# Five places instead of six for the weights of a layer change, and a V half that stays on the chip

## The chip, the cores and the metric

One core of a Trainium2 chip runs the kernel. The metric is the device time of one execution in microseconds (us), lower is better. Three runs of the kernel before gave 176.09, 176.46 and 176.43 us, a median of 176.43. One further execution was taken with the hardware profiler; it took 176.3 us, of which the instructions span 174.6 us. All times of single instructions come from that execution and are counted from the start of its span.

Five engines work side by side: TensorE (PE, matmuls; the profile shows its weight loads as PEld), VectorE (DVE), ScalarE (ACT), GpSimd (POOL) and SyncE (SP), which here only issues the transfers from the chip's main memory (HBM). The on-chip memories are SBUF, where loads land, and PSUM, eight banks that hold the results of matmuls.

## The reference

One token for each of 4 sequences goes through four layers: attention A, gated network B, then A and B again **with the same weights and the same cache**. Cut to what matters:

```python
def A(x):                               # x: 4 x 1 x 512
    q = (x @ wq)                        # 512 x 4096: 32 heads of 128
    k, v = last 2048 keys of each of 8 kv heads (4 query heads share one)
    p = softmax(q k^T / sqrt(128))
    return (p v) @ wo                   # 4096 x 512
def B(x):
    return (sigmoid(x @ w_gate) * (x @ w_up)) @ w_down   # 512 x 1792, 1792 x 512

x = x + A(layernorm(x)); x = x + B(layernorm(x))
x = x + A(layernorm(x)); x = x + B(layernorm(x))
```

K and V are 16 MB each (bf16), wq and wo 4 MB each, the three B matrices 1.75 MB each.

## The kernel before, in words

**Memory.** SBUF is cut into 50 half tiles of 512 KB (128 partitions x 2048 bf16). All of K, 32 half tiles, stays from the first attention to the second, so K is read once. The other 18 half tiles are a pool of nine whole tiles for V, wq, wo and the B weights. A tile of V holds one kv head for two of the four sequences: it is named by the head and by the pair, (head, 0) or (head, 1). The 2048 keys of a sequence lie 32 on each of 64 partitions; so each half of a V tile has 16 key blocks, 128 elements wide, on every partition.

**The two attentions.** The first (`attn_first`) takes the heads 0 to 7, the second (`attn_second`) 7 to 0, so that the last tiles of V can serve both. (7, 0) and (7, 1) do; (6, 1) waits in four PSUM banks meanwhile (`stash`, line 580, and `load_stash`, line 595, both transposes on DVE). The rest of V is loaded again.

**The layer change.** Between the two attentions lie the first B and the projection of q. Their weights are 18 loads of 256 to 512 KB: four quarters each of w_gate and w_up (448 KB), four parts of w_down (384 to 512 KB), and six of the eight 512 KB parts of wq, written (quarter of the rows, half of the columns); two parts of wq stay from the first attention. The pool has no free tile then, since wo's four tiles and V are held. So these loads go into **places**, half tiles that the first attention has just left:

- WQ and WR: the tiles that held the first two row quarters of wq. Their second halves keep the wq parts that stay. The first halves, (WQ, 0) and (WR, 0), then hold the two halves of the V tile (6, 0).
- Y: the tile of (6, 1), empty after the stash: (Y, 0) and (Y, 1).
- Z: the tile of (7, 0); its first half waits in PSUM in the meantime (`stash_half`, line 602) and so (Z, 0) is empty.
- SP: half a tile's worth of small buffers (`side`), not needed in between.

A load is named with its place by `load_half` (line 505 to 516). `load_wq`, `load_glu` and `load_v` list the loads in order. All transfers are issued on SP, in exactly that order (line 400): a load waits there until the last reader of its place is done, and those behind it wait too. The order of instructions on the other engines is made by a planner (`_schedule`) from estimated durations; behind the second norm, TensorE's order is fixed as written.

**V tile (6, 0).** In the first attention its half 0 is in (WQ, 0), half 1 in (WR, 0). Of half 0, 11 of the 16 key blocks are put aside: 7 in a PSUM bank as f32 pairs (`save_part`, a DVE transpose, line 639), 4 in the buffer of a constant, `permo` (`save_rest`, an ACT copy, line 644). For the second attention, `restore_part` brings them into (WR, 1) by an ACT copy and a DVE transpose (lines 650 and 652), and GpSimd builds the constant anew (line 658). The other 5 blocks of half 0 (160 KB, the load named `PART`) and the whole half 1 (512 KB) are loaded again.

**Fillers.** `keep_op` and `add_zeros` (lines 783 ff.) issue matmuls that add nothing to what is read later. They stand where TensorE would wait.

**The end.** In the last B (`glu` with `last=True`), two w_gate tiles and two w_up tiles are multiplied (line 1484), DVE transposes the result (1496), ACT and DVE form the gate, and w_down is multiplied in three pieces (line 1533). `x_rows` puts x into the same PSUM bank ahead of that (line 1468).

Of the kernel before, what the change touches and what calls it, by code (L numbers as in the profile page):

```python
# [6 lines left out]
F32 = mybir.dt.float32  # L7
BF16 = mybir.dt.bfloat16
ACTF = mybir.ActivationFunctionType
ALU = mybir.AluOpType  # L10
# [268 lines left out]
def build(nc, A_x, A_k, A_v, A_wq, A_wo, B_wg, B_wu, B_wd, out, cfg=None):  # L279
# [14 lines left out]
    REP = HQ // HKV  # L294
# [30 lines left out]
    with es:  # L325
# [99 lines left out]
        WR = ("wq", 1, 0)  # L425
        RET = ("ret",)
        PART = ("Vh", 0, HKV - 2, 0, 1)
        SP = ("side",)
        base = {SP: SIDE}

# [95 lines left out]
        def load_wq(k):  # L526
            if k == 0:
                for c in range(NC):
                    load(("wq", c, k), 2, "bw_8k", (2 * SLOT, wq_d[:, c, :], False))
            else:  # L530
                for c, i, place in ((2, 1, (WR, 0)), (3, 1, (Y, 0)), (0, 0, (SP, 0)), (1, 0, (Y, 1)), (2, 0, (WQ, 0)), (3, 0, (Z, 0))):
                    load_half(("wq", c, k, i), wq_d[:, c, i * SLOT:(i + 1) * SLOT], "bw_4k", SLOT, place)

        def wq_part(k, c, i):
# [21 lines left out]
        def load_glu(k):  # L556
            for nm, src, two in (("wg", wg_d, wg_p), ("wu", wu_d, wu_p)):
                if k == 0:
                    for c in range(NC):
                        load_half((nm, c, k), src[:, c, :], "bw_3k", F,  # L560
                                  (((WR, 0), (Y, 0), (SP, 0), (Y, 1)), ((WQ, 0), (Z, 0), (WR, 0), (Y, 0)))[nm == "wu"][c])
                    continue
                for cc in range(NC // 2):
                    load((nm, cc, k), 2, "bw_8k", (2 * F, two[:, cc, :], False))
            for n, (a, b) in enumerate(bounds_of(k)):
                if k == 0:
                    load_half(("wd", a, k), wd_d[:, a:b, :].rearrange("p k n -> p (k n)"), "bw_4k", (b - a) * D,
                              ((SP, 0), (Y, 1), (WQ, 0), (Z, 0))[n])
# [44 lines left out]

        def load_v(h, bp, k, n_use):
            name = ("V", h, bp, k)
            tiles = ({(HKV - 2, 0): ((WR, 1), (WR, 0)), (HKV - 3, 1): ((Y, 0), (Y, 1))} if k
                     else {(HKV - 2, 0): ((WQ, 0), (WR, 0))}).get((h, bp))
            if tiles is not None:
                halves[h, bp] = []
                for n, tile in enumerate(tiles):  # L620
                    half = ("Vh", n, h, bp, k)
                    load_half(half, pair_d(A_v, h, bp)[:, :, n * SLOT:(n + 1) * SLOT], "bw_4k", SLOT, tile, SAVED if half == PART else 0)
# [12 lines left out]
        def saved_f(s):  # L635
            return slot_ap(s)[:, SAVED_S:SAVED].bitcast(F32)

        def save_part(s):
            P.op("vector", "sv1", c_dve(SAVED_P), lambda v: v.transpose(saved_p, saved_f(s)),
                 r=[("slot", s)], w=[("sv", 1)], banks=(CB,))  # L640

        def save_rest(after):
            s = base[WQ]
            P.op("scalar", "sv0", c_act(SAVED_S), lambda a: a.copy(permo[:, :], slot_ap(s)[:, 0:SAVED_S]),
                 r=[("slot", s)], w=[("permo",)], after=after)
            give(s)

        def restore_part():
# [3 lines left out]
            b = P.op("vector", "rv1", c_dve(SAVED_P), lambda v: v.transpose(saved_f(s), saved_p),  # L652
                     r=[("sv", 1)], w=[("rv", 1)], banks=(CB,), after=tuple(fresh))
            for o in (a, b):
                o.deps.update(saved["deps"])
            for m in range(REP):
                P.op("gpsimd", "permo2%d" % m, 300.0,
                     lambda g, m=m: g.affine_select(permo[:, m * 128:(m + 1) * 128].rearrange("p (r v) -> p r v", r=REP),
                                                    one[:, 0:1].broadcast_to([128, 128]).rearrange("p (r v) -> p r v", r=REP),
                                                    [[0, REP], [-4, 32]], ALU.is_equal, 0.0, base=-m, channel_multiplier=1),  # L660
                     r=[("one",)], w=[("permo",)])

        on_free[Y] = lambda s: hfree.update((s, s + 1))

# [139 lines left out]
        def layer_norm(tag, b0, b1, for_q, add=None):  # L804
# [362 lines left out]
        def pv_wide(tag, h, k2, tiles):  # L1167
# [6 lines left out]
            def e_pv(pe):  # L1174
                last = None
                for n in range(4):
# [5 lines left out]
                                         src.rearrange("p (m t d) -> p t m d", t=2, d=128)[:, t], start=(n == 0), stop=(n == 3))  # L1182
                return last
            P.op("tensor", "PV" + tag, 16 * tm["pe_row"], e_pv,
                 r=[("slot", x) for x in ss.values()] + [("e", k2)] + [("rv", n) for n in range(2) if h == HKV - 2],
                 w=[("pso", k2, 0), ("pso", k2, 1)], banks=(ob,))
            for bp, _ in tiles:
                for name in sorted(set(x[0] for x in parts[bp]), key=str):
# [111 lines left out]
        def attn_first():  # L1300
            def front(h):
                k_transpose(h)
                softmax_unit("0.%d" % h, h)
                turn = lambda: turn_p(0, "0.%d" % h, h % 2, PBS[h % 2])
                return turn

            for h in range(2):
                front(h)()
            for h in range(HKV):
                tag = "0.%d" % h  # L1310
                turn = front(h + 2) if h + 2 < HKV else None
                if h == HKV - 1:
                    need(Z)
                    so0 = stash_half(0, named("oq0.%d" % (h - 1)))
                op = pv_unit(tag, h, h % 2, v_tiles[(0, h)])
                if h == HKV - 2:
                    oe, oq = named("oe" + tag), named("oq" + tag)
                    oe[0].deps.add(stash(stashed, (0, 1)))
                    oq[0].deps.add(stash(stashed, (2,), oe))
                    st = stash(stashed, (3,), oq)  # L1320
                if h == HKV - 1:
                    named("oe" + tag)[0].deps.update((st, so0))
                    for o in P.ops:
# [3 lines left out]
                    save_rest(tuple(named("pm" + tag)))  # L1327
# [117 lines left out]
        def glu(k, b0, b1, add=None, last=False):  # L1445
# [29 lines left out]
            for n, nm in enumerate(("wg", "wu")):  # L1475
                for c in range(NC):
# [3 lines left out]
                    def e_g(pe, c=c, s=s, n=n):  # L1480
                        last = None
                        src = slot_ap(s) if k == 0 else tile_ap(s)[:, c % 2 * F:(c % 2 + 1) * F]
                        for g in range(4):
                            last = pe.matmul(ps[32 * g:32 * g + NB, gub[n], 0:NF], xn[:, c * NB:(c + 1) * NB],  # L1484
                                             src[:, g * NF:(g + 1) * NF], start=(c == 0), stop=(c == NC - 1),
                                             skip_group_check=True)
# [210 lines left out]
```

## Time and profile before

| what | value |
|---|---|
| median of 3 runs | 176.43 us (176.09 to 176.46) |
| the profiled execution | 176.3 us |
| its span | 174.6 us |
| PE, DVE, ACT, POOL busy | 114.9, 105.9, 34.0, 23.1 us |
| bytes read from HBM | 69.37 MB |
| stretches of the span | first attention to about 105 us, layer change to about 122, second attention to about 162, last B to the end |

The page of the profile gives busy time by engine, the busy share in 40 slices of the span (one digit each, 9 is 90% or more; a slice is 4.4 us), the DMA queues, and groups of instructions by line. Further views used below: the chain of waits (the work that ended last, followed back; start, length, what), the timeline (start, length, engine, line, operation, output<-input, and in brackets the idle time before it and what ended that), the view by stretches (busy us and number of instructions by engine, granted TensorE clock, share of the DMA engines' time, GB/s), and the DMA view, which gives the time from a load's issue to its landing.

### The profile page before, as it was taken

How to read it: one execution, taken by the hardware profiler on the slowest of the kernel's cores; microseconds unless marked ns; L12 is line 12 of the kernel's file. 1: busy time of each engine (PE TensorE's matmuls, PEld its weight loads, DVE VectorE, ACT ScalarE, POOL GpSimd, SP SyncE). 2: the span in 40 equal slices, each digit the busy share in tenths (PEclk: the TensorE clock that was granted, in tenths of full speed). 3: DMA queues.
4: the chain of work that ended last, by engine and by line, in shares of the span. 5: the costliest groups of instructions: out<-in, count | busy, mean ns of one | idle time of the engine just before them, and what ended most of it. 6: DMA issues, size and time to landing. Idle time of an engine off the chain costs nothing.

```text
span 174.6 us, 3997 instructions
## 1 busy us (share of the span) xinstructions
PE 114.9 (66%) x1686; PEld 58.6 (34%) x1698; DVE 105.9 (61%) x262; ACT 34.0 (19%) x89; POOL 23.1 (13%) x92
## 2 busy tenths in 40 slices
PE   0536237167557092569788788767958999879853
PEld 0203012013434051243467552243323434446311
DVE  6407997994866938469323732316598999751531
ACT  2002022312212103011021010102233545430101
POOL 6100010101100101001010000002011543442000
PEclk9999999999999999999999999999999999999975
DMA  5999999999999999999999999999999999999970
GB/s 189 420 428 430 422 420 420 408 423 420 420 419 409 424 420 420 420 412 421 420 408 425 412 395 407 407 409 405 407 413 417 422 417 420 417 424 420 415 319 26
DMA packets 12370, 69.64 MB, mean 399 GB/s; under 512 B 1336, under 2 KB 1472, under 8 KB 6336
## 3 DMA queue, kind: packets, MB, share of 16 engines
q1 hardware_dynamic: 12344, 69.38, 97.0%
q8 instruction: 13, 0.21, 0.5%
q14 instruction: 5, 0.04, 0.1%
q10 hardware_dynamic: 8, 0.00, 0.0%
HBM read 69.37 MB, written 0.00 MB: 397 GB/s over the span
## 4 chain that ended last, share of the span: by engine, by line
DMA 71%; PE 11%; DVE 7%; SPq 6%; issue 1%; ACT 1%; POOL 0%; DVEq 0%
DMA arena<-in_A_v_cache_dram 49%; DMA arena<-in_B_w_down_dram 15%; SPq L400 6%; DMA side<-in_A_wq_dram 4%; DMA arena<-in_B_w_up_dram 4%; PE ps L783 2%; PE ps L1088 2%; DVE arena L595 1%; PE ps L986 1%; PE ps L1091 1%; PE ps L1181 1%; DVE small L1001 1%; ACT side L1016 1%; PE ps L1289 1%; DVE arena L1191 1%
## 5 line engine op out<-in xcount | busy, mean ns | idle before, releaser
L956 DVE STREAM_TRANSPOSE arena<-arena 128x1024 f32<-128x1024 f32 x32 | 37.0, 1205 | 0.1
L986 PE MATMUL ps<-arena,side 128*32 128x512 bf16 x256 | 23.3, 494 | 0.3
L1001 DVE TENSOR_REDUCE small<-ps 128x1 f32<-128x512 f32 x16 | 10.9, 679 | 15.8 <-PE ps L986 15.8
L783 PE MATMUL ps<-perm 128*128 128x448 bf16 (+1 forms) x65 | 18.5, 397 | 1.0 <-DVE side L1496 0.8
L1016 ACT ACTIVATE side<-ps,small 128x512 bf16<-128x512 f32 x16 | 11.0, 687 | 35.7 <-PE ps L1115 18.5
L973 PE MATMUL ps<-small,perm 128*128 128x512 bf16 x16 | 7.7, 482 | 12.0 <-DVE arena L956 11.3
L1088 PE MATMUL ps<-side,arena 128*128 128x64 bf16 x320 | 11.3, 192 | 4.0 <-DMA arena<-in_A_v_cache_dram 4.0
L1091 PE MATMUL ps<-side,arena 128*128 128x8 bf16 x256 | 8.1, 168 | 8.8 <-DMA arena<-in_A_v_cache_dram 8.7
L949 ACT CAST side<-ps 128x256 bf16<-128x256 f32 x16 | 5.9, 371 | 33.6 <-PE ps L986 26.6
L1088 PEld LDWEIGHTS ps<-side,arena 128*128 128x128 bf16 x320 | 10.2, 97 | 6.3 <-DMA arena<-in_A_v_cache_dram 6.3
L1031 ACT CAST side<-ps 128x512 bf16<-128x512 f32 x16 | 9.4, 587 | 12.6 <-PE ps L1289 2.9
L1045 POOL CAST small<-small 128x1 bf16<-128x1 f32 x9 | 1.7, 188 | 76.0 <-ACT side L1016 76.0
L1091 PEld LDWEIGHTS ps<-side,arena 128*128 128x128 bf16 x256 | 7.4, 104 | 11.6 <-DMA arena<-in_A_v_cache_dram 9.0
L986 PEld LDWEIGHTS ps<-arena,side 128*32 128x32 bf16 x256 | 6.3, 108 | 11.7 <-issue 8.7
L897 PE MATMUL ps<-arena,xn 128*4 128x512 bf16 x60 | 6.5, 498 | 4.2 <-DMA arena<-in_A_wq_dram 4.2
L1105 DVE TENSOR_TENSOR onb<-ps,rinv 128x16 bf16<-128x16 f32 x9 | 1.7, 185 | 11.4 <-PE ps L1088 10.8
L944 PE MATMUL ps<-side,eyew 32*128 32x64 bf16 x64 | 5.4, 212 | 4.3 <-ACT side L949 2.4
L1036 DVE STREAM_TRANSPOSE side<-side 128x256 f32<-128x256 f32 x16 | 6.9, 433 | 2.0 <-ACT side L1031 1.8
L1181 PE MATMUL ps<-arena,side 128*32 128x512 bf16 x112 | 7.3, 380 | 0.8 <-ACT side L1016 0.4
L783 PEld LDWEIGHTS ps<-perm 128*128 128x128 bf16 x65 | 5.9, 110 | 5.3 <-issue 2.9
L1496 DVE STREAM_TRANSPOSE side<-ps 128x448 f32<-128x448 f32 x4 | 2.6, 651 | 7.9 <-PE ps L1484 7.9
L1484 PE MATMUL ps<-arena,xn 128*4 128x448 bf16 x60 | 4.7, 360 | 3.1 <-DMA arena<-in_B_w_up_dram 2.7
(138 smaller groups left out, 151.1 us busy)
## 6 DMA issues: line engine op xcount, KB each, us to landing
arena<-in_A_v_cache_dram SPq DMA_DIRECT2D x26, 1024.0 KB, 16.6
arena<-in_A_k_cache_dram SPq DMA_DIRECT2D x16, 1024.0 KB, 24.9
arena<-in_A_wq_dram SPq DMA_DIRECT2D x4, 1024.0 KB, 7.8
arena<-in_A_wo_dram SPq DMA_DIRECT2D x3, 1024.0 KB, 26.6
arena<-in_A_v_cache_dram SPq DMA_DIRECT2D x5, 512.0 KB, 8.6
arena<-in_A_wq_dram SPq DMA_DIRECT2D x5, 512.0 KB, 6.7
arena<-in_B_w_up_dram SPq DMA_DIRECT2D x4, 448.0 KB, 6.1
arena<-in_B_w_gate_dram SPq DMA_DIRECT2D x2, 896.0 KB, 20.7
```

What stands on the lines that cost most here:

```text
L400: o = P.op("sync", name, 0.0, lambda e, dst=dst, src=src: e.dma_start(dst, src), r=r, w=w, dma_bytes=nbytes, dma_rate=tm[rate])
L783: last = pe.matmul(dst, weights, src, start=False, stop=False, skip_group_check=True)
L956: P.op("vector", "T%d_%d" % (h, t), c_dve(1024), lambda v, v32=v32: v.transpose(v32, v32), r=[("slot", 4 * h + t)], w=[("slot", 4 * h + t)])
L973: last = pe.matmul(ps[:, bank, :], perm[:, :], msk_m[:, :].unsqueeze(1).broadcast_to([128, 256, 2]), start=True, stop=False)
L986: last = pe.matmul(ps[32 * gi:32 * gi + 32, bank, :], qbd[:, q0:q0 + 32], kt[:, cp // 2, cp % 2, jh * NJ:(jh + 1) * NJ, :], start=False, s ...
L1001: lambda v: v.tensor_reduce(nmax[:, k2:k2 + 1], ps[:, bank, :], AXX, ALU.max),
L1016: lambda a: a.activation(prow[:, :].rearrange("p (m x t) -> p m x t", x=32, t=2), ps[:, bank, :].rearrange("p (m t x) -> p m x t", x=32, t ...
L1031: P.op("scalar", "pc" + tag, c_act(512), lambda a: a.copy(prow[:, :], ps[:, pb, :]), r=[("ppb", pb)], w=[("prow",)], banks=(pb,))
L1036: P.op("vector", "pt" + tag, c_dve(256), lambda v: v.transpose(et, prow[:, :].bitcast(F32)), r=[("prow",)], w=[("e", k2)])
L1088: last = pe.matmul(ps[:, ob, o:o + 64], v, ef[:, j % 2, at - at % 64:at - at % 64 + 64], start=(j == 0), stop=(j == 2 * NJ - 1), skip_grou ...
L1091: last = pe.matmul(ps[:, ob, bp * 8:bp * 8 + 8], v, ev[:, j % 2, j % 16 // 2, x0:x0 + 8], start=(j == 0), stop=(j == 2 * NJ - 1))
L1181: last = pe.matmul(ps[32 * g:32 * g + 32, ob, :], ew[:, g, mq, t], src.rearrange("p (m t d) -> p t m d", t=2, d=128)[:, t], start=(n == 0) ...
```

## The change

The places of the layer change are dealt anew, five instead of six: (WR, 0) is no longer among them. Half 1 of the V tile (6, 0) stays in it from the first attention to the second (`KEPT`) and isn't loaded again. Of half 0, only what goes into PSUM is put aside, 480 f32 columns instead of 448, which is 7.5 key blocks instead of 11; the copy into `permo` and back, and the rebuilding of `permo`, are gone. The `PART` load grows accordingly and is put into the list one place earlier, ahead of the last wq part. The halves of the V tile (5, 1) get other places. Some filler matmuls are added, dropped or moved.

```diff
         PART = ("Vh", 0, HKV - 2, 0, 1)
+        KEPT = ("Vh", 1, HKV - 2, 0, 0)
...
-                for c, i, place in ((2, 1, (WR, 0)), (3, 1, (Y, 0)), (0, 0, (SP, 0)), (1, 0, (Y, 1)), (2, 0, (WQ, 0)), (3, 0, (Z, 0))):
+                for c, i, place in ((2, 1, (Y, 1)), (3, 1, (SP, 0)), (0, 0, (Z, 0)), (1, 0, (WQ, 0)), (2, 0, (Y, 0)), (3, 0, (Y, 1))):
+                    if place == (Y, 1) and i == 0:
+                        load_half(PART, pair_d(A_v, HKV - 2, 0)[:, :, 0:SLOT], "bw_4k", SLOT, (WR, 1), SAVED)
                     load_half(("wq", c, k, i), wq_d[:, c, i * SLOT:(i + 1) * SLOT], "bw_4k", SLOT, place)
...
-                                  (((WR, 0), (Y, 0), (SP, 0), (Y, 1)), ((WQ, 0), (Z, 0), (WR, 0), (Y, 0)))[nm == "wu"][c])
+                                  (((WQ, 0), (Y, 0), (Y, 1), (SP, 0)), ((Z, 0), (WQ, 0), (Y, 0), (Y, 1)))[nm == "wu"][c])
...
-                              ((SP, 0), (Y, 1), (WQ, 0), (Z, 0))[n])
+                              ((SP, 0), (Z, 0), (WQ, 0), (Y, 0))[n])
...
+            if k and (h, bp) == (HKV - 2, 0):
+                halves[h, bp] = [(PART, 0), (KEPT, 0)]
+                return
-            tiles = ({(HKV - 2, 0): ((WR, 1), (WR, 0)), (HKV - 3, 1): ((Y, 0), (Y, 1))} if k
+            tiles = ({(HKV - 3, 1): ((Z, 0), (WQ, 0))} if k
...
-        SAVED_S, SAVED_P = REP * 128, 7 * 64
-        SAVED = SAVED_S + 2 * SAVED_P
+        SAVED_P = 480
+        SAVED = 2 * SAVED_P
...
-        def save_rest(after):
-            s = base[WQ]
-            P.op("scalar", "sv0", c_act(SAVED_S), lambda a: a.copy(permo[:, :], slot_ap(s)[:, 0:SAVED_S]),
-                 r=[("slot", s)], w=[("permo",)], after=after)
-            give(s)
...
-            a = P.op("scalar", "rv0", c_act(SAVED_S), lambda a: a.copy(slot_ap(s)[:, 0:SAVED_S], permo[:, :]),
-                     r=[("permo",)], w=[("rv", 0)])
...
-            for m in range(REP):
-                P.op("gpsimd", "permo2%d" % m, 300.0,
...
-                keep_op("kw" + tag, 2, WB, 0, 512)
+                keep_op("kw" + tag, 2 - (tag == "G0"), WB, 0, 512)
...
-                            add_zeros(pe, 3 if c == 2 - 2 * n else 2, WB, NF)
+                            add_zeros(pe, 3 if n or c == 2 else 2, WB, NF)
...
+                    if last and n and c == 1:
+                        x_rows()
+                        keep_op("kwJ", 2, SB[0], 0, 448)
...
             if last:
-                x_rows()
-                keep_op("kwI", 2, SB[0], 0, 448)
+                keep_op("kwI", 3, SB[0], 0, 448)
...
-            keep_op("kw2", 2, WB, 0, 512)
+            keep_op("kw2", 1, WB, 0, 512)
```

So the 18 loads go into these places, in order:

| | w_gate 0-3 | w_up 0-3 | w_down 0-3 | wq |
|---|---|---|---|---|
| before | WR, Y0, SP, Y1 | WQ, Z, WR, Y0 | SP, Y1, WQ, Z | WR, Y0, SP, Y1, WQ, Z |
| after | WQ, Y0, Y1, SP | Z, WQ, Y0, Y1 | SP, Z, WQ, Y0 | Y1, SP, Z, WQ, Y0, Y1 |

The wq parts come in the order (2,1), (3,1), (0,0), (1,0), (2,0), (3,0).

More of the change, by code (lines that the diff above doesn't have):

```diff
@@ L621, in load_v @@
                     half = ("Vh", n, h, bp, k)
-                    load_half(half, pair_d(A_v, h, bp)[:, :, n * SLOT:(n + 1) * SLOT], "bw_4k", SLOT, tile, SAVED if half == PART else 0)
+                    load_half(half, pair_d(A_v, h, bp)[:, :, n * SLOT:(n + 1) * SLOT], "bw_4k", SLOT, tile)
+                    left[half] += half == KEPT
                     if half == ("Vh", 0, HKV - 2, 0, 0):
@@ L628, in load_v @@
             load(name, n_use, "bw_8k", (2 * SLOT, pair_d(A_v, h, bp), True))
-        SAVED_S, SAVED_P = REP * 128, 7 * 64
-        SAVED = SAVED_S + 2 * SAVED_P
+        SAVED_P = 480
+        SAVED = 2 * SAVED_P
         saved_p = ps[:, CB, 0:SAVED_P]
         def saved_f(s):
-            return slot_ap(s)[:, SAVED_S:SAVED].bitcast(F32)
+            return slot_ap(s)[:, 0:SAVED].bitcast(F32)
         def save_part(s):
@@ L640, in save_part @@
                  r=[("slot", s)], w=[("sv", 1)], banks=(CB,))
-        def save_rest(after):
-            s = base[WQ]
-            P.op("scalar", "sv0", c_act(SAVED_S), lambda a: a.copy(permo[:, :], slot_ap(s)[:, 0:SAVED_S]),
-                 r=[("slot", s)], w=[("permo",)], after=after)
-            give(s)
+            hfree.add(s)
         def restore_part():
             s = need(PART)
-            a = P.op("scalar", "rv0", c_act(SAVED_S), lambda a: a.copy(slot_ap(s)[:, 0:SAVED_S], permo[:, :]),
-                     r=[("permo",)], w=[("rv", 0)])
-            b = P.op("vector", "rv1", c_dve(SAVED_P), lambda v: v.transpose(saved_f(s), saved_p),
+            o = P.op("vector", "rv1", c_dve(SAVED_P), lambda v: v.transpose(saved_f(s), saved_p),
                      r=[("sv", 1)], w=[("rv", 1)], banks=(CB,), after=tuple(fresh))
-            for o in (a, b):
-                o.deps.update(saved["deps"])
-            for m in range(REP):
-                P.op("gpsimd", "permo2%d" % m, 300.0,
[L658 to L661, printed above, removed]
+            o.deps.update(saved["deps"])
         on_free[Y] = lambda s: hfree.update((s, s + 1))
@@ L1184, in pv_wide @@
             P.op("tensor", "PV" + tag, 16 * tm["pe_row"], e_pv,
-                 r=[("slot", x) for x in ss.values()] + [("e", k2)] + [("rv", n) for n in range(2) if h == HKV - 2],
+                 r=[("slot", x) for x in ss.values()] + [("e", k2)] + [("rv", 1) for _ in range(h == HKV - 2)],
                  w=[("pso", k2, 0), ("pso", k2, 1)], banks=(ob,))
@@ L1326, in attn_first @@
                     so = stash_half(1, named("oq" + tag))
-                    save_rest(tuple(named("pm" + tag)))
                     give(base[Z])
```

## The prediction

> **What bounds the kernel now.** I read the page's slices first, then the queues and the issues.
>
> ```profile
> DMA  5999999999999999999999999999999999999970
> GB/s 189 420 428 430 422 420 420 408 423 420 420 419 409 424 420 420 420 412 421 420 408 425 412 395 407 407 409 405 407 413 417 422 417 420 417 424 420 415 319 26
> q1 hardware_dynamic: 12344, 69.38, 97.0%
> arena<-in_A_v_cache_dram SPq DMA_DIRECT2D x5, 512.0 KB, 8.6
> arena<-in_A_wo_dram SPq DMA_DIRECT2D x2, 256.0 KB, 10.5
> arena<-in_A_v_cache_dram SPq DMA_DIRECT2D x1, 160.0 KB, 5.9
> ```
>
> The transfers are busy from the second slice to the third last, the layer change (slices 23 to 28, at 395 to 409 GB/s) included: there is no hole to fill, and a load costs its bytes over the rate. The last two lines name what the change touches: 160 KB is the V part that comes back beside one of the 512 KB halves.
>
> Next, the chain of waits in order of time, and TensorE's timeline of the end:
>
> ```profile
> 115.54 6.23 DMA side<-in_A_wq_dram
> 121.77 0.04 issue
> 121.82 0.39 PE ps L897 x4
> ...
> 144.13 26.99 DMA arena<-in_B_w_down_dram
> ```
>
> ```profile
> 165.27 0.55 PE L1484 MATMUL ps<-arena,xn 128*4 128x448 bf16 x8
> 167.46 0.69 PE L1484 MATMUL ps<-arena,xn 128*4 128x448 bf16 x8 [1.64 <-DMA arena<-in_B_w_up_dram]
> 167.92 0.65 PE L1468 MATMUL ps<-side,xT 128*4 128x128 f32 x8
> 168.51 0.93 PE L783 MATMUL ps<-perm 128*128 128x448 bf16 x2
> 169.93 1.02 PE L1533 MATMUL ps<-arena,rinv 128*4 128x128 bf16 x32 [0.49 <-DMA arena<-in_B_w_down_dram]
> 171.16 1.02 PE L1533 MATMUL ps<-arena,rinv 128*4 128x128 bf16 x24 [0.21 <-DMA arena<-in_B_w_down_dram]
> ```
>
> Three stretches follow. Up to 121.8 us TensorE takes each weight as it lands. From 121.82 to the w_gate matmuls at 163.91 nothing of weight waits for a load (the only DMA wait of TensorE's there is 0.3 us): this is computing, with loads up to 11 us ahead. From 165.8 on everything waits for a landing again: 1.64 us for the second w_up tile, then three times for w_down. The last load was issued 20 us before it landed, so **the end is set by bytes in the queue**. Earlier bytes bring it forward until computing is late.
>
> **The change, part by part.** Times are those of the profiled execution: span 174.6, 176.3 us in all. The median of the runs is 176.43, 0.13 above it.
>
> *Bytes.* One V half (512 KB) is no longer loaded a second time: it stays in (WR, 0). Of the other half 7.5 blocks instead of 11 wait in PSUM, so 2048 - 960 = 1088 elements of 2 B on 128 rows come back, 272 KB instead of 160. Net 512 - 112 = 400 KB, 409,600 B. In the stretch where they go, 120 to 125 us, the view by stretches gives 408 GB/s: 1.00 us. Rows of 2,176 B aren't dearer: the two 256 KB pieces of wo, in 2,048 B rows, land 0.65 us apart, 403 GB/s. Term: **-0.99 us** (-1.28 for the half, +0.29 for the larger part).
>
> The part's rows now begin 1,920 B into a run, before 2,816 B. The Trainium skill (DMA: Bandwidth & Descriptors, How a descriptor splits into AXI transactions) cuts reads at 256 B boundaries; by it 1,920 is off a boundary and 2,816 was on one, which by estimate makes 9 pieces of 8.5, 0.04 us against the change. No row here shows a misaligned load alone.
>
> *One place less.* Eighteen loads of the layer change (8 of w_gate and w_up, 4 of w_down, 6 of wq) went round six places and now go round five. A place's next load waits on SP for the matmul that empties it, and all later loads queue behind it on SP. What counts is the lead: how long before the previous landing a load is issued.
>
> ```profile
> 100.42 0.33 SPq L400 DMA_DIRECT2D arena<-in_B_w_gate_dram  x1
> 104.33 3.19 SPq L400 DMA_DIRECT2D arena<-in_B_w_up_dram  x4
> ```
>
> By the DMA view of single issues, the load at 100.42 lands 8.5 us later, at 108.9; the next goes out at 104.33, a lead of 4.6, the shortest here. The wq load at 115.54 lands at 121.77 (chain), the one before it a 512 KB step of 1.28 earlier: lead 4.9. I redo this with five places: w_up 0 takes Z at 104.7 (freed by the vector copies, as before) against 108.9, lead 4.2; w_up 1 takes WQ when w_gate 0's matmul ends at 106.37, against 110.0: **3.6, the shortest**; the rest come to 3.7 to 4.5, as each lead loses one load, 1.1 to 1.3 us. What lead is needed? The first load, on empty queues, lands 4.8 us after its issue, of which 2.48 is its 1 MB at 423 GB/s: 2.3 us of latency. Leads of 3.6 cover that by 1.3. From below, no lead under 4.6 was run, so 4.6 is the other end. I take 2.3, a measured start, and cost the place at 0.
>
> *The order on SP.* The V part is now issued ahead of the last wq part (3,0). Its place, (WR, 1), is empty when q's second matmul ends, about 120.0; (3,0) needs the third, just after. SP waits no longer than before: the part was issued at 120.13. But (3,0) lands behind 272 KB: 125.6 + 0.7 = 126.4. Its matmul runs at 127.78, 1.4 us later: hidden. Without that cover each us late is a us on DVE's chain. The V halves of head 5 wait for (0,0) and (1,0) to be used, 122.2 and 123.5, with leads of 4.1. Wq (0,0), which starts the computing stretch, has the same bytes before it: 121.77 stands.
>
> *Copies.* Gone are ACT's two copies (0.62 each, at 103.69 and 120.13) and POOL's four selects (1.45 in all). The first held back w_up 0 until 104.33, in a queue that stayed full; the others have idle engines around them. DVE's two transposes grow from 448 to 480 columns, 651 to some 700 ns, and DVE idles 2.3 and 1.6 us soon behind them. Sum 0. A late restore would move head 6's product, first needed after 135.
>
> *Filler matmuls.* One less in the first norm, one less ahead of w_down 0, two more behind w_up 1 and 2: these run at 0.19 each where TensorE waits for landings (w_up 2's last ends near 113.40, the load lands at 113.43). Cost 0, bounds -0.2 and +0.1. At the end the x rows and two fillers move ahead of the wait for the second w_up tile, one filler is added behind it. These are read with the clock, whose windows I laid at 3.41 us steps back from its fall:
>
> ```profile
> 126.78:130.20 3.42, 2.19 (x29) 1.00 1.04 411
> ...
> 164.33:167.74 3.41, 1.65 (x30) 1.00 1.02 419
> 167.74:171.16 3.42, 2.72 (x50) 0.50 0.53 208
> ```
>
> After 2.19 us of work in a window the clock stays full, after 1.65 it is halved. The moved matmuls add about 1 us to the latter, so I expect the clock to hold to the end. The last 8 matmuls, 0.41 us at half speed, would take 0.35 by the nearest full-speed row (8 of L879), the 16 before them a little less: **-0.1 us**, between 0 and -0.2. Could the fillers be late? With loads 0.99 earlier the second w_up tile lands at 166.43. TensorE ends the first at 165.7, then 0.35 and 0.4 of moved work: 166.45. Then 0.55, DVE's 0.65 and 0.22 and their hops: hT near 168.4, while w_down lands at 168.89. All of the 0.99 passes, with 0.5 to spare.
>
> The Trainium skill (TensorE: Matmul & The Clock Gate, Why this matters for your kernels) asks for an idle gap of about 3 us before the clock falls. Here it fell after idle pieces of at most 1.64 us, so the trace differs. By that rule the moved matmuls change nothing and the sum is -0.99 instead of -1.09.
>
> *Sum*: -0.99 - 0.1 = -1.1: 176.3 becomes 175.2, and on the median's footing **175.3 us**.
>
> **The rivals.**
>
> 1. *The queue runs dry (slower).* If a load needs the 4.6 us of lead that the trace proves, five places with a mean lead near 4.05 lose 0.55 for each round of five; 18 loads are 3.6 rounds, 2.0 us. Less the 1.1 saved: +0.9, **177.3**. It decides once the needed lead passes 4.05 by 0.3. For it: no shorter lead was ever run, and every matmul that empties a place waits for a landing itself. Against it: the first load's 2.3 us.
>
> 2. *Computing takes the gain.* The stretch from 121.8 to 163.9 keeps its length, so only 0.5 us of slack is left before hT is late. A window in the layer change has 2.34 us of TensorE work (113.13 to 116.54) and loses about 0.25: 2.1, just under the lowest that held. If the clock falls there, 1.4 us of matmuls after 121.8 double, and further windows follow: 1 to 1.5 us late, less 0.5 of slack, eats 0.5 to 1.0: **176.1**. Against: 2.1 is nearer 2.19 than 1.65.
>
> 3. *The bytes don't come off the last transfer.* From 167.74 to 171.16 the DMA share is 0.53: some of the 16 engines are done early, and the last ones set the end. A half is spread over all, so each loses a sixteenth. Were the last engine held by something else, the gain would be the clock's alone: **176.3**.
>
> **How the numbers follow.** Forecast 0.60, its own range 174.8 to 175.8. Computing takes the gain 0.13 (0.05 of it still faster). Bytes not off the last engine 0.05. Dry queue 0.17. The rest, 0.05, is a gain of up to 1.7 us, should the copies taken off ACT and POOL count after all. A run of this kernel tells 0.2%, 0.35 us, from no change: faster is under 176.08. Faster 0.60 + 0.05 + 0.05 = 0.70; same 0.08 + 0.05 = 0.13; slower 0.17. The range goes from 174.7 (that gain, on the median's footing) to 176.6 (computing at its worst, and the spread of the runs), which leaves out the dry queue.
>
> **What would show it.** Right: 68.97 MB in the queue line, DMA slices without a digit under 9 between 104 and 131 us, wq (0,0) landing near 121.8, w_gate of the last layer again near 163.9, the last landing near 170.7, a clock row without a 5 at its end. Wrong: DMA under 0.95 in a stretch from 104 to 131 (dry queue), a w_gate start past 164.5 (computing), or w_down's last landing unmoved (last engine).

## The result, and the profile after

The changed kernel takes **177.22 us** (median of 20 runs, 176.07 to 178.72), the kernel before on the same chip 176.29 (20 runs, 176.09 to 176.52). The ratio is 1.006, with a 95% interval of 1.0043 to 1.0078: **slower**, where 175.3 was forecast. The kernel before repeats within 0.4 us, the changed one spreads over 2.6. (Medians here are over all runs; the ratios leave out runs more than 1.5% above the fastest of their kernel.) The profiled execution took 178.67 us, span 176.9, against 176.3 and 174.6; it is the second slowest of the 20, so its holes are larger than those of the median.

The page of the changed kernel, the same rows as shown of before, with the clock and the chain's shares ahead and behind:

```profile
PEclk9999999999999999999999999999699999999995
DMA  5999999999999999999999999999999999999970
GB/s 181 432 426 424 422 428 417 406 424 422 426 411 415 422 419 426 415 410 429 419 411 419 407 402 403 393 393 341 370 298 372 430 417 430 415 422 413 427 307 10
q1 hardware_dynamic: 12200, 68.97, 96.2%
DMA 45%; DVE 27%; PE 22%; issue 2%; ACT 1%; SPq 1%; POOL 0%; DVEq 0%
```

Of the kernel before, the last of these rows reads:

```profile
DMA 71%; PE 11%; DVE 7%; SPq 6%; issue 1%; ACT 1%; POOL 0%; DVEq 0%
```

The bytes came out as worked out: 68.97 MB instead of 69.38. But in the slices 28 to 31 the rate is 298 to 372 GB/s, where it was 405 to 417 before. The DMA row keeps its nines all the same: **a packet counts as busy from its start to its end, however long it stands**. Packets of 4 KB, which take 0.16 us in the kernel before, take up to 2.2 us here, so the hole shows in GB/s only. And the chain now runs through computing for about half of its length (DVE 27%, PE 22%), where that was a fifth (7% and 11%).

By stretches (width, busy times, granted clock, DMA share, GB/s), the changed kernel and then two stretches of the kernel before:

```profile
112.00:116.00 4.00, 2.99 (x43) 1.51 (x42) 0.86 (x2) 0.00 (x0) 0.00 (x0) 1.00 1.01 392
116.00:120.00 4.00, 3.03 (x54) 1.51 (x49) 1.05 (x7) 0.00 (x0) 0.00 (x0) 1.00 1.04 390
120.00:124.00 4.00, 1.78 (x17) 0.69 (x13) 2.88 (x5) 0.38 (x2) 0.00 (x0) 1.00 1.00 335
124.00:128.00 4.00, 3.91 (x35) 1.22 (x37) 0.84 (x2) 0.74 (x2) 0.00 (x0) 0.57 1.01 371
128.00:132.00 4.00, 2.63 (x41) 0.99 (x38) 3.82 (x9) 1.64 (x4) 0.70 (x3) 1.00 0.95 312
132.00:136.00 4.00, 3.11 (x39) 1.16 (x33) 3.29 (x13) 1.15 (x3) 0.59 (x2) 1.00 0.87 338
```

```profile
120.00:124.00 4.00, 3.04 (x37) 1.17 (x33) 2.84 (x5) 1.37 (x4) 1.25 (x4) 1.00 1.03 409
128.00:132.00 4.00, 3.08 (x36) 1.24 (x28) 3.73 (x12) 1.06 (x4) 1.00 (x4) 1.00 1.00 413
```

From 104 to 136 us the mean of the eight stretches is 368 GB/s against 408.5. Over 32 us that is 1.29 MB not moved, 3.2 us at the old rate; less the 0.99 us of bytes saved, 2.2. The two executions are 2.37 apart. So the loss is found, and nearly all of it is in this stretch.

TensorE's timeline of the changed kernel at the start of the second attention:

```profile
120.84 0.39 PE L890 MATMUL ps<-side,xn 128*4 128x512 bf16 x4 [0.66 <-DMA side<-in_A_wq_dram]
121.16 0.39 PE L842 MATMUL ps<-small 128*128 128x4 f32 x2
123.11 0.39 PE L890 MATMUL ps<-arena,xn 128*4 128x512 bf16 x4 [1.57 <-DVE arena L652]
125.15 1.90 PE L979 MATMUL ps<-arena,side 128*32 128x512 bf16 x16
```

The matmul at 123.11 uses wq (0,0). The profile names DVE's restore (L652), which ended at 123.07, but in the kernel before that matmul ran at 121.82 and the restore after it, from 122.57: the matmul doesn't need it. Of the kernel before:

```profile
121.82 0.39 PE L897 MATMUL ps<-side,xn 128*4 128x512 bf16 x4 [0.60 <-DMA side<-in_A_wq_dram]
122.57 0.65 DVE L652 STREAM_TRANSPOSE arena<-ps 128x448 f32<-128x448 f32 x1
123.64 1.09 PE L986 MATMUL ps<-arena,side 128*32 128x512 bf16 x16
```

In the changed kernel (0,0) is the first of the three loads issued from 116.22 on, and the DMA view of that issue gives 6.9 us to its landing:

```profile
116.22 2.48 SPq L400 DMA_DIRECT2D arena<-in_A_wq_dram  x3
arena<-in_A_wq_dram SPq DMA_DIRECT2D x1, 512.0 KB, 6.9
```

So it landed at 123.1, 1.3 us later than before, and **the matmul waits for its load**. The clock is then halved (0.57 above), and the first scores take 1.90 us instead of 1.09. By the order of events K's half tiles then come free late and V's loads are issued late, which makes the second hole, at 128 to 136; e9 below tests whether the clock matters in that.

### The profile page after: what moved, and what is told of

It reads as the page before. It is cut to its first block, busy times and chain, and to the rows that moved or that the text cites. A ratio compares the mean times of both kernels' runs of the same rounds, so it can differ in the third digit from the quotient of the medians.

```text
span 176.9 us, 3998 instructions
## 1 busy us (share of the span) xinstructions
PE 116.6 (66%) x1689; PEld 59.1 (33%) x1701; DVE 106.1 (60%) x262; ACT 32.7 (18%) x87; POOL 21.7 (12%) x88
## 3 DMA queue, kind: packets, MB, share of 16 engines
q1 hardware_dynamic: 12200, 68.97, 96.2%
## 4 chain that ended last, share of the span: by engine, by line
DMA 45%; DVE 27%; PE 22%; issue 2%; ACT 1%; SPq 1%; POOL 0%; DVEq 0%
DMA arena<-in_A_v_cache_dram 18%; DMA arena<-in_B_w_down_dram 18%; DVE arena L949 12%; PE ps L979 8%; DMA arena<-in_A_wq_dram 6%; DVE small L994 3%; DMA arena<-in_B_w_up_dram 3%; PE ps L966 3%; PE ps L1081 2%; PE ps L776 2%; DVE small L998 1%; DVE arena L598 1%; PE ps L1084 1%; PE ps L1174 1%; PE ps L890 1%
## 5 line engine op out<-in xcount | busy, mean ns | idle before, releaser
L979 PE MATMUL ps<-arena,side 128*32 128x512 bf16 x256 | 24.1, 509 | 0.1
L846 ACT ACTIVATE small<-ps 128x4 f32<-128x4 f32 x4 | 0.7, 174 | 46.7 <-PE ps L842 46.7
L1174 PE MATMUL ps<-arena,side 128*32 128x512 bf16 x112 | 7.3, 380 | 0.8 <-ACT side L1009 0.4
```

The costliest lines, as they stand in the source:

```text
L979: last = pe.matmul(ps[32 * gi:32 * gi + 32, bank, :], qbd[:, q0:q0 + 32], kt[:, cp // 2, cp % 2, jh * NJ:(jh + 1) * NJ, :], start=False, s ...
L1174: last = pe.matmul(ps[32 * g:32 * g + 32, ob, :], ew[:, g, mq, t], src.rearrange("p (m t d) -> p t m d", t=2, d=128)[:, t], start=(n == 0) ...
```

## The experiments

"Places" are those of the layer change. A load's *lead* is, as in the prediction, from its issue to the landing before it.

**1. Is a load more or less the cause? e1_reload.** The changed kernel, but half 1 loaded again.

```diff
-                halves[h, bp] = [(PART, 0), (KEPT, 0)]
+                halves[h, bp] = [(PART, 0), (("Vh", 1, HKV - 2, 0, 1), 0)]
...
+                load_half(("Vh", 1, HKV - 2, 0, 1), pair_d(A_v, HKV - 2, 0)[:, :, SLOT:2 * SLOT], "bw_4k", SLOT, (WR, 0))
```

> The changed kernel, but half 1 of the V tile is loaded a second time, into (WR, 0), where it lies already. The load stands ahead of the first wq part, and its place is long empty, so it waits for nothing and adds its 1.28 us to the lead of every load behind it. Theory of the dry queue (five places leave leads of about 3.7 us, and that is too little): the queue stays full and the time is that of the bytes: 176.3 + 0.3 (the larger part) - 0.1 = 176.5 us, with a spread of a few tenths, although 512 KB more are moved than in the changed kernel. Rival (the queue isn't what costs; fillers, the clock or the longer rows do): 1.28 us more than the changed kernel, 178.5 us, with its wide spread.

Measured 179.62 us (178.4 to 180.6), ratio 1.0185 (1.0152 to 1.0218). The theory missed by 3 us, and the rival's 178.5 is too low by 1.1. It seems that a load that needs no place doesn't fill the queue for good but only puts its own bytes ahead. In the trace the second part of w_down already loses 1.0 us (lead 3.73), before that load can help; (3,1) then loses 1.2 with a lead of 6.0, which the lead at its own issue doesn't explain.

**2. Six places again: e2_sixth, and mended e2b_sixth.** Half of the K tiles of head 7 serves as a sixth place. The kernel leaves out that head's K in the second attention: the first scores there are formed from head 6's K, by the same instructions.

```diff
-        base = {SP: SIDE}
+        X = ("K7",)
+        base = {SP: SIDE, X: 4 * (HKV - 1)}
...
-                  r=[("msk_m",)] + perms + [("slot", 4 * hk + t) for t in range(4)] + [("q", k2)],
+                  r=[("msk_m",)] + perms + [("slot", 4 * kk + t) for t in range(4)] + [("q", k2)],
```

> The changed kernel with six places: a half of K's tile of head 7 serves as the sixth once the first attention has scored that head, and the loads go round as in the kernel before. It leaves out K of head 7 in the second attention: those scores are formed from head 6's K, same shapes and instructions. The V half stays on the chip, the part has 7.5 blocks, all fillers are those of the change. Theory of the dry queue: with the lead of before, the gain forecast appears: 175.2 us, spread a few tenths, wq (0,0) lands near 121.8 us, and no 5 in the clock row ahead of the end. Rival (fillers, clock or rows): about 177.2 us, as the changed kernel.

Measured 177.64 us (176.01 to 180.58), 1.005 (1.0024 to 1.0076). All 18 loads landed as before, but TensorE then waited 2.87 us for the restore (L652): the first scores no longer waited for head 7's K, so the planner put other DVE work ahead of it. That is a side effect of the experiment, so it decided nothing. In e2b_sixth the scores wait for both heads' slots, and the order is the changed kernel's:

```diff
-[("slot", 4 * kk + t) for t in range(4)]
+[("slot", 4 * x + t) for x in sorted({kk, hk}) for t in range(4)]
```

> The changed kernel with six single places again at the layer change: one half of the K tiles of head 7 serves as the sixth, so the first scores of the second attention are taken from the K tiles of head 6 (that part of the computation is replaced; instructions, waits on both heads' slots and bytes stay as in the changed kernel, and the order of DVE and PE is the changed kernel's). V's half 1 is still kept, the part of half 0 is loaded behind the last wq part. Theory (five places leave the queue too short at 112 to 122 us): loads land as in the kernel before, wq (0,0) at 121.9, clock held, and the 400 KB saved show: 175.3 us (175.1 to 175.6). Rival (the queue is disturbed by something else than the number of places, or the restore of the part disturbs the start of the attention): 176.5 us or more.

Measured **175.25 us** (175.03 to 177.97, 10 of 12 within 175.03 to 175.40), ratio 0.9946 (0.9932 to 0.9961). With six places the saved bytes show: 1.08 us less than the kernel before on the same chip (176.33) by the medians and 0.95 by the ratio, where the bytes are worth 0.99. Its stretches, in which the rate drops behind the layer change only:

```profile
120.00:124.00 4.00, 3.04 (x34) 1.07 (x29) 2.95 (x5) 0.75 (x3) 0.00 (x0) 1.00 1.02 407
128.00:132.00 4.00, 3.03 (x35) 1.22 (x33) 3.73 (x12) 1.06 (x4) 0.99 (x4) 1.00 0.94 388
```

**3. The fillers: e3_before_fill** (the kernel before with the change's fillers) **and e4_after_fill** (the reverse).

```diff
-                keep_op("kw" + tag, 2, WB, 0, 512)
+                keep_op("kw" + tag, 2 - (tag == "G0"), WB, 0, 512)
...
+                    if last and n and c == 1:
+                        x_rows()
+                        keep_op("kwJ", 2, SB[0], 0, 448)
```

> The kernel before with the change's filler matmuls alone (one less in the first norm and ahead of w_down, one more behind two w_up parts, x rows and two fillers ahead of the last w_up tile, three in place of two behind it). Theory of the dry queue: no loss, and the clock holds to the end: 176.2 us, between 176.0 and 176.4. Rival (the fillers let the clock fall at the layer change): 176.8 or more, with a half-speed window near 117 to 125 us.

> The changed kernel with the fillers of before. Theory of the dry queue: it stays slow and scattered, 177.2 us (176.5 to 178), since the leads are the same. Rival (the fillers cost): 175.4 us.

Measured 176.33 us (ratio 1.0005, 0.9996 to 1.0014) and 178.11 us (1.0089, 1.0055 to 1.0124). In e3 the fillers cost between -0.1 and 0.25 us by the interval, so they don't cause the loss, and without them (e4) it stays. In e3 the clock held to the end, and that was worth nothing that shows either.

**4. Five places with the rest as before: e6_five_places and e7_part_last.** e7 moves the load of half 0's part behind the last wq part; e6 also loads half 1 again behind it.

```diff
                 for c, i, place in ((2, 1, (Y, 1)), (3, 1, (SP, 0)), (0, 0, (Z, 0)), (1, 0, (WQ, 0)), (2, 0, (Y, 0)), (3, 0, (Y, 1))):
-                    if place == (Y, 1) and i == 0:
-                        load_half(PART, pair_d(A_v, HKV - 2, 0)[:, :, 0:SLOT], "bw_4k", SLOT, (WR, 1), SAVED)
                     load_half(("wq", c, k, i), wq_d[:, c, i * SLOT:(i + 1) * SLOT], "bw_4k", SLOT, place)
+                load_half(PART, pair_d(A_v, HKV - 2, 0)[:, :, 0:SLOT], "bw_4k", SLOT, (WR, 1), SAVED)
```

> The changed kernel, but half 1 of the V tile is loaded again at the place in the order that the kernel before gives it (part of half 0, then half 1, both behind the last wq part). So it has five places and 112 KB more bytes than the kernel before. Theory (five places cost the time): the changed kernel's time plus one load of 512 KB, 1.25 us: 178.4 us (177.6 to 179.2). Rival (the loss comes from where the part of half 0 now stands, not from five places): 0.3 us of bytes above the kernel before, 176.6 us (176.4 to 176.9).

> The changed kernel with one load moved: the part of V's half 0 behind the last wq part instead of ahead of it. Five places, half 1 kept, 7.5 blocks kept. Theory (five places): no better than the changed kernel, 177.0 us (176.3 to 178.5), wq (0,0) landing late again. Rival (the part's load ahead of the last wq part disturbs the queue): 175.4 us (175.2 to 175.7).

Measured 179.15 us (176.68 to 180.72; ratio 1.0066, 1.0042 to 1.0091) and 176.83 us (175.55 to 178.99; 1.0026, 1.0004 to 1.0047). For e6 both figures lie above the 176.6 of its rival, so the loss is there also when the part's load stands behind the last wq part. e7 differs from e2b_sixth in the places, and in the head whose K the first scores read: **five places instead of six cost 1.6 us** (1.4 by the ratios). What e7 has less than the change, 0.4 us to its 177.22, could be the part's place in the order, but that isn't shown: on another chip the same changed kernel took 178.3 (e13 below).

**5. The second hole: e9_hold_clock.**

```diff
             q_mms(1, 1, WB, range(NC))
+            P.op("tensor", "kwZ", 5 * 223.0, lambda pe: add_zeros(pe, 5, WB, 512), w=[("qrow", 1)], banks=(WB,))
             variance()
```

> The changed kernel with five products of zeros (512 columns, 1.1 us at the full clock) on PE behind the last product of the first q half, where PE waits for wq (0,0). Queue, places and bytes are untouched. Theory of an amplifier (the wait for wq (0,0) drops the clock, the first scores then take 1.9 instead of 1.1 us, and the K slots come free late enough to empty the queue a second time): the clock holds through 122 to 128, the loads behind V(5,1) are issued up to 2 us earlier, 176.4 us (176.1 to 176.7) with little scatter. Rival (the first loss alone, or the slow packets themselves, set the time): 177.2 us, as scattered as the changed kernel.

Measured 177.31 us (176.61 to 180.81), 1.0048 (1.0026 to 1.007). The median is the rival's, and the ratio's interval overlaps that of the change (1.0043 to 1.0078), so the amplifier isn't shown to add to the loss. With the clock at 1.00 from 120 to 132 in its profiled execution, which is its fastest, the holes are smaller but still there:

```profile
120.00:124.00 4.00, 3.52 (x31) 1.31 (x30) 3.01 (x7) 0.38 (x2) 0.00 (x0) 1.00 0.96 357
128.00:132.00 4.00, 2.46 (x31) 1.01 (x32) 3.86 (x9) 1.24 (x4) 0.70 (x3) 1.00 1.01 351
```

**6. Where the sixth place is needed: e10_five_in_wq, e11_six_in_wq, e12_sixth_part_first,** beside **e13_after_again**. All but the last are e2b_sixth with other tables, here e10's and e11's:

```diff
-((2, 1, (X, 0)), (3, 1, (Y, 0)), (0, 0, (SP, 0)), (1, 0, (Y, 1)), (2, 0, (WQ, 0)), (3, 0, (Z, 0)))
+((2, 1, (Y, 0)), (3, 1, (SP, 0)), (0, 0, (Y, 1)), (1, 0, (WQ, 0)), (2, 0, (Z, 0)), (3, 0, (Y, 0)))
...
+((2, 1, (X, 0)), (3, 1, (Y, 1)), (0, 0, (SP, 0)), (1, 0, (Z, 0)), (2, 0, (WQ, 0)), (3, 0, (Y, 0)))
```

> The changed kernel with a sixth place (half of the K tiles of head 7; the first scores of the second attention are taken from head 6's K tiles in its stead, that part is replaced) for the loads of w_gate, w_up and w_down alone; the wq parts go round the five others. Theory (a load loses when it is issued less than about 4.6 us ahead of the landing before it, wherever that happens): no loss up to the last w_down part, then leads near 3.8 to 4.3 us for wq (2,1), (3,1), (0,0) and 0.6 to 2 us lost there: 176.7 us (176.0 to 177.8), scattered. Rival (the loss comes from the weights' stage and is only seen later): as with six places throughout, 175.3 us.

> The same with the sixth place for the wq parts alone; w_gate, w_up and w_down go round the five others. Same part of the computation replaced. Theory: leads of 3.7 to 4.3 us from the second part of w_up to the last of w_down, where the traces with five places lost 0 to 1.0 us at the second part of w_down, and 4.6 us or more from then on, no loss: 175.7 us (175.2 to 176.4). Rival (a fifth place less in any stage costs the same): 176.8 us.

> Six places throughout as in the kernel with the sixth place (same part of the computation replaced), and the part of V's half 0 ahead of the last wq part, as in the change. Theory (its place in the order costs only where the queue is short): 175.3 us (175.1 to 175.6). Rival (that place costs by itself, through its own issue or its rows of 2176 bytes): 175.7 us or more.

> The changed kernel once more, on the same chip and beside the other three, so that their distances from it are from one call. All theories: 177.2 us (176.9 to 177.5), scattered from 176 to 179; above the kernel with the part behind the last wq part (176.83 us) if its place in the order costs with five places, the same if not.

- **e10**: 176.6 us (175.77 to 179.35; ratio 1.001, 0.9985 to 1.0034), as the theory had it.
- **e11**: 178.54 us (176.64 to 179.59; 1.0093, 1.0057 to 1.0129), 2.8 above its theory and no better than the change beside it (e13). Part of that is the new table: V (5,1)'s first half now waits for (1,0)'s matmul and goes out at 125.36 with a lead of 2.4, and the stretch 124 to 128 falls to 273 GB/s. The rest is lost at wq parts with leads of 5 to 7.
- **e12**: 175.87 us (175.14 to 178.45; 0.9983, 0.996 to 1.0006). Even with six places the part's place in the order costs 0.6 us (0.7 by the ratios, whose intervals just touch). In e2b_sixth (3,0) goes out at 118.6, but here it stands on SP behind the part until 120.85: its lead is 4.3 instead of 5.9, and 120 to 124 falls from 407 to 367 GB/s.
- **e13**: 178.3 us (176.68 to 178.72; 1.0096, 1.0065 to 1.0126), 1.1 above the 177.2 that every theory expected. It is the changed kernel itself, so for these scattered kernels a difference of up to a microsecond between two chips says little; e10 and e12 lie 1.7 and 2.4 below it on the same chip.

**7. The leads alone: e14_six_late, e15_six_late_glu, e16_before_late.** No place, byte or order of loads changes, and in the traces VectorE, ScalarE, GpSimd and TensorE run the same instructions in the same order (matmul records that are missing from one trace or the other left aside). Loads wait for one product more, as they would with five places. e15 ends at w_down (12 for 18), e16 is the kernel before.

```diff
+        parts = [("wg", c, 0) for c in range(NC)] + [("wu", c, 0) for c in range(NC)] + [("wd", a, 0) for a, _ in bounds_of(0)]
+        parts += [("wq", c, 1, i) for c, i in ((2, 1), (3, 1), (0, 0), (1, 0), (2, 0), (3, 0))]
+        users = ["glwg0_%d" % c for c in range(NC)] + ["glwu0_%d" % c for c in range(NC)] + ["gd0_%d" % a for a, _ in bounds_of(0)] + ["q1_1_2"]
+        for n in range(5, 18):
+            named(str(parts[n]))[0].deps.update(named(users[n - 5]))
```

> The kernel with the sixth place throughout (half of the K tiles of head 7, whose part in the first scores of the second attention is replaced by head 6's), all tables, bytes and orders left, but each load from the second part of w_up to the last wq part waits for one product later than its place needs, as it would with five places. So places, their addresses and the bytes are those of a kernel of 175.25 us, and the leads those of five places (3.6 to 4.3 us). Theory (the lead is what costs): as with five places and the part behind the last wq part, 176.8 us (176.2 to 177.6), scattered. Rival (what costs is which places the loads go to, or how the places alternate): 175.3 us (175.1 to 175.6).

> The same with the later waits from the second part of w_up to the last part of w_down alone; the wq parts are issued as soon as their places are free, with leads of about 5 us. Theory (short leads starve the DMA engines that run ahead of the slowest one; the landings stay on time until that reserve of 0.6 of a load is used up, and the loss shows two to four loads later, whatever their leads): 177 us (176.3 to 178.6), the run-ahead near 0 by the first wq part. Rival (a load loses by its own lead alone): 175.5 us (175.2 to 175.9).

> The kernel before, whole and with its own six places, bytes and blocks kept, with the same later waits from the second part of w_up to the last wq part. Theory: 1.6 to 2.0 us more than the kernel before, 178.1 us (177.4 to 179.2), scattered. Rival (places, not leads): 176.3 us.

Measured 177.57 us (175.99 to 179.38; ratio 1.0052, 1.003 to 1.0074), 176.54 (175.67 to 178.74; 1.0012, 0.9989 to 1.0034) and 177.87 (176.7 to 179.72; 1.0069, 1.0045 to 1.0093), all three in the ranges of their theories. **It is the lead**: the places of a kernel of 175.25 us give 177.57 with it shortened, and those of the kernel before 176.26 give 177.87. e14's stretches show holes of the same kind as the change's. The clock fell in them too, so not all of its loss need be the queue's:

```profile
116.00:120.00 4.00, 2.49 (x46) 1.62 (x46) 0.04 (x1) 0.00 (x0) 0.00 (x0) 0.83 0.95 368
120.00:124.00 4.00, 3.81 (x26) 1.53 (x26) 2.56 (x9) 0.00 (x0) 0.00 (x0) 0.50 0.85 285
```

Against 175.25, short leads in the weights' stage alone cost 1.3 us (e15), in wq alone 1.35 (e10), in both 2.3 (e14); by the ratios these are 1.2, 1.1 and 1.9.

Worked out from the issues and landings of each profiled execution, for the loads issued from 104 us to the last wq part (a step is the time from one landing to the next; 1.1 to 1.3 us where nothing is lost):

```
kernel      leads, us                   longest steps, us    median, us
before      4.60 to 5.90                1.33                 176.3
e2b         5.05 to 5.85                1.39                 175.25
change      3.71 to 4.58 up to (0,0)    2.27, 1.74           177.22
e7          3.69 to 4.76 up to (1,0)    1.97, 1.85           176.83
e10         3.83 to 5.45                1.68, 1.67           176.6
e15         3.72 to 5.88                1.84, 1.75           176.54
e14         3.10 to 5.39                2.50, 2.05           177.57
e16         3.67 to 5.08                2.09, 1.86           177.87
```

## Why the prediction was wrong

**Bytes: right.** 68.97 MB, and 175.25 us in the kernel that keeps the old leads through the layer change, against a forecast of 175.3. None of the saving was lost at the last engine (rival 3).

**One place less: this step failed.** It worked out leads of 3.6 to 4.5 us, which the trace of the change shows (3.71 to 4.58), and set against them a need of 2.3 us, the latency of the first load on empty queues. So it put the place at 0, where five places cost 1.4 to 1.6 us (e7 against e2b_sixth). That leads of this size cost time is shown by e14 and e16. Why they do is worked out from single traces: the need is more, for two reasons, the second of which the trace of before already held:

- *The latency under load is longer.* The trace doesn't name the engine of a packet, but a packet that starts just as a completion packet ends is the first of a load on that engine. In e7 six such packets, which take 0.16 us otherwise, stand at the same time, until 118.06 to 118.62. The latest load that can be is (3,1), issued at 115.37, since the next went out at 116.83 only, less than 2.3 us ahead: so at least 2.7 to 3.3 us from issue to data. In the change one stands until 122.21, and by the same count its load was issued no later than 118.37: 3.8 us. The Trainium skill (DMA: Bandwidth & Descriptors, Specifications) gives about 0.6 us to the first byte for transfers issued from SP; by that figure, or by my 2.3, no lead here was short. On the empty queues of the kernel before the trace agrees with it: the first packet starts at 1.81 us, 0.6 after the end of its issue and 1.0 after the start. Under load it is the 2.7 us and more of these packets.
- *A landing is that of the slowest of 16 engines, and the others are ahead of it.* Counting the engines' completion packets at each landing gives a mean advance of 0.5 to 0.9 of a load from w_up to (0,0), in the kernel before and in e2b_sixth; at the wq parts it is 0.56 of a load, or 0.7 us, before and 0.50 in e2b_sixth. The lead of an engine that is ahead is shorter by its advance. In the change that advance melts to 0.19 of a load by wq (2,1)'s landing, in e7 to 0.00 by (0,0)'s. Packets put together to one line for each engine leave engines idle for up to 1.0 us at a time in the change, from 107.9 us on; in the kernel before the longest such gap between 4 and 168 us is 0.05 us. As long as the advance lasts, the landings look undisturbed, and so, by this account, the loss shows some loads late.

Together, by estimate, a mean engine needs a lead of 3.4 to 4.0 us (2.7 to 3.3 and the advance of 0.7), and those furthest ahead need more. In the kernels that kept every lead of these loads at 4.6 or more no load was late. With leads of 3.6 to 4.6 some were and others not, which fits the scatter.

**The rival.** The dry queue was priced at 177.3 from 4.6 us, the shortest lead that the trace proved, and given 0.17. I had put both ends side by side and taken the one measured on an empty queue. The nearest row was the other: same stage, same load, same rate. That its 177.3 meets the measured 177.22 is in part luck: the same kernel took 178.3 on another chip (e13), and its mechanism as put, that each round of five places loses what the lead lacks, is not what runs. The loss is irregular, and in the profiled execution a good part of it lies in the second hole, which the rival didn't have.

**The order on SP: off in size.** It was costed at 0, as (3,0) could wait. With six places it costs 0.6 us (e12). With five, (3,0) has to wait for its place anyway, and whether the part's load costs the 0.4 us between e7 and the change isn't shown.

**Copies, fillers, clock.** The fillers cost 0 (e3), and e2b_sixth, without the copies, leaves no room for a cost of theirs. The last term was off: the clock at the end, -0.1, is worth 0 (e3), and in the change it fell at the end all the same. The reading behind it, that a window with 2.19 us of work keeps the clock and one with 1.65 doesn't, agrees with the changed kernel, where 2.09 kept it and 1.60 didn't:

```profile
113.77:117.18 3.41, 2.09 (x44) 1.00 1.01 402
120.60:124.01 3.41, 1.60 (x13) 1.00 0.96 337
124.01:127.42 3.41, 3.41 (x31) 0.50 1.02 388
```

Computing (rival 2) is late only behind the holes: w_gate's matmuls of the last layer start at 166.22 instead of 163.91.

**The signs.** "DMA under 0.95 in a stretch" would have missed the first hole, whose share is 1.00, and the nines in the DMA row, a sign of being right, came true although the queue ran dry. The GB/s row, or (0,0)'s landing at 123.1 instead of 121.8, shows it.

**Open.** Around 120 to 122 us many packets take 0.3 to 2 us, in every kernel with short leads in the weights' stage, in e1, e11 and e15 at loads with leads of 5 to 6 us as well. Some are the first of a load (in the change two of 2.0 and 1.4 us), but in e11 nearly all stand in the middle of one. The advance explains that only in part: it had melted in e11 (0.06 of a load) but not in e1 (1.06). So a load's own lead doesn't tell whether that load is late. A kernel that keeps half 1 *and* leads of 4.6 us should beat both, as e2b_sixth suggests, but that one gives up head 7's K; I found no sixth place that is free, so none was run.

## What to carry to other kernels

When a change takes a buffer out of a ring of prefetches, compare the new lead with the shortest lead that the same stage has been seen to survive, not with the latency on an empty queue; here 4.6 us survived and 3.7 didn't, and one buffer was 1.1 to 1.3 us of lead. A saved byte is worth its time only while the queue stays full: the change that saves 400 KB gained 1.1 us with six buffers and lost 0.9 with five. Look for a starved queue in bytes per second, not in its share of busy time, and a few loads ahead of the first late landing.

## What the runs showed beyond that

- The clock row shows a 9 also where the trace holds no record of the clock. In the profiled execution of e12 the record begins at 43.9 us and has half clock from 47.3 to 81.5, the fives below. In the kernel before it begins at 82.4 only:

```profile
PEclk9999999999955555556999999999999999999995
PEclk9999999999999999999999999999999999999975
```

But the same 16 matmuls of scores take as long there in the kernel before (second line) as in e12 (first line), against 1.09 us at 123.64:

```profile
51.62 1.90 PE L981 MATMUL ps<-arena,side 128*32 128x512 bf16 x16
51.57 1.90 PE L986 MATMUL ps<-arena,side 128*32 128x512 bf16 x16
```

So TensorE was as slow there before the change too, and the nines ahead of 82 us say nothing. All windows of the clock read in this document lie behind that.

- One short lead can be enough, or not: in the eleven profiled kernels with five places' leads at the second part of w_down, a lead of 3.70 to 3.81 us there came with a step of 1.62 to 2.50 us in eight and of 1.24 to 1.27 in three.
